# Moving the cluster choice on VectorE to other places in its queue, with its products and the last conversions

## The chip, the cores and the metric

The kernel runs on one core of one Trainium2 chip. The metric is the device time of one execution in microseconds (us), median over runs. Five engines work side by side, each through its own queue in order: PE (TensorE: matmuls and transposes), DVE (VectorE), ACT (ScalarE), POOL (GpSimd), and SP (SyncE), which here only starts DMAs.

## The reference, cut to what matters

Clustered attention over 2 batches, 8 heads, 768 positions of 64, followed by two feed-forward networks (the second one gated). A query only sees the keys of its own cluster:

```python
q_assign = np.argmax(np.einsum('bhsd,hcd->bhsc', q_n, c_n), axis=-1)   # 16 centroids per head
k_assign = np.argmax(np.einsum('bhsd,hcd->bhsc', k_n, c_n), axis=-1)
mask = q_assign[:, :, :, None] == k_assign[:, :, None, :]
scores = np.where(mask, scale * np.matmul(q, k.transpose(0, 1, 3, 2)), -1000000000.0)
attn = np.exp(scores - np.max(scores, axis=-1, keepdims=True))
attn = attn / (np.sum(attn, axis=-1, keepdims=True) + 1e-09)
x = np.matmul(attn, v)
...
h = x @ w_in;  x = (h * (1.0 / (1.0 + np.exp(-h)))) @ w_out
gate = 1.0 / (1.0 + np.exp(-(x @ w_gate)));  out = gate * (x @ w_val) @ w_out
```

## The kernel before

**Pairs and tiles.** Attention runs over 8 pairs (a batch and two heads, p = 0 to 7), a pair over 12 tiles of 128 queries: tiles i = 0 to 5 belong to the first head, named 0_0 to 0_5, tiles 6 to 11 to the second, 1_0 to 1_5. Every product is done from high and low parts. A tile goes through this chain: scores s (PE, L442, four matmuls into one of two PSUM buffers), their negated maximum nm (DVE, L450), the exponential e with the row's sum into tot (ACT, L455), six transposes of e (PE: two into u, L469, and four into t, L478), and copies of u and t into the ring ph (L66, L63; u on DVE, t on DVE or ACT). After three tiles a value group v is done (PE, 12 matmuls, L486); its halves are added by way of other (ACT, L495) and xf (DVE, L498). There are two buffers for s, so the scores of a tile wait for the exponential two tiles back.

**The order on PE** is written by hand (`tc.manual_schedule`): one_tile issues the scores of tile i+2, a due value group at every third tile, pieces of the next pair's preparation, the transposes of tile i, and a step of finishing the previous pair. The table PIECES says how many pieces go ahead of and behind the transposes of each tile. The order on the other engines is decided by the scheduler; `tc.issue_after(x)` keeps an instruction behind x. The list maxima holds all nm, 12 to a pair: index 0 is nm_0_0, index 4 nm_0_4, index 7 nm_1_1, index 11 nm_1_5.

**Preparing the next pair (prep)**, piece by piece: splits of q and k into high and low parts (POOL), products with the centroids pm (PE) and their scaled copy sim (ACT, L271), similarities ps (PE, L162) and a second copy into sim (ACT, L63), and then the *choice* on DVE: mk, the largest similarity of each position (L406); eq, where it is (L409); wq, eq times a rank (L412); the largest of those into mk again (L414), named mk2 below; oh, the one-hot choice (L416). The choice is transposed to pt (PE, L425), copied to rows (ACT, L427) and brought into the mask rows of q and k by four DMAs (L429, L430). The scores of the next pair need these rows.

**Finishing a pair (finish)**: tot + 1e-9 and its reciprocal rs (DVE, L504, L506), a transpose pr (PE, L508), rt (ACT, L510), out to DRAM and back as a broadcast rb (two DMAs, L577, L579), and the product acc (POOL, L516), which is the pair's part of the MLP's input.

**The last pair** has nothing to prepare. There the first MLP weights are converted: converted() takes 64-bit words from DMA tiles (ri, ro) by an ACT operation (L679), a clamp on POOL (L680) and three DVE operations (L685, L687, L689). The first four such tiles are ci_0, ci_1, co_0 and co_1; the list behind ties each of their 12 DVE operations to one maximum of the last pair. From ci_0 and ci_1 come sums si (POOL, L724 to L727) and high and low parts wi0a, wi0b, wi0s, wi0t (high: ACT, L63; low: POOL, L697), from co the parts wo. Behind 255 us only the MLPs run.

Of the kernel before, what the change touches and what calls it, by code (L numbers as in the profile page):

```python
# [15 lines left out]
ALU = mybir.AluOpType  # L16
AX = mybir.AxisListType
# [14 lines left out]
def clustered_attention_then_two_mlps(ctx, tc, qT, kT, v, cen, cenT, w1i, w1o, w2g, w2v, w2o, out):  # L32
    nc = tc.nc
    B, HP, _, S = qT.shape
    D = cen.shape[2]
    H = 2 * HP
    C = cenT.shape[3]
# [70 lines left out]
    with ExitStack() as att:  # L108
# [259 lines left out]
        def prep(p):  # L368
# [34 lines left out]
            yield  # L403
            W = 4 * NT
            sg = sim.rearrange("p t n j c -> p (t n j) c")
            nc.vector.tensor_reduce(mk[:, 0, :], sg, axis=AX.X, op=ALU.max)  # L406
            yield
            eq = wk.tile([P, W, C], BF16, tag="eq", name=f"eq{p}", bufs=1)
            nc.vector.tensor_tensor(eq, sg, mk[:, 0, :].unsqueeze(2).to_broadcast([P, W, C]), op=ALU.is_equal)  # L409
            yield  # L410
            wq = wk.tile([P, W, C], BF16, tag="wq", name=f"wq{p}", bufs=1)
            nc.vector.tensor_tensor(wq, eq, mk[:, 2, 0:C].unsqueeze(1).to_broadcast([P, W, C]), op=ALU.mult)  # L412
            yield
            nc.vector.tensor_reduce(mk[:, 1, :], wq, axis=AX.X, op=ALU.max)  # L414
            o = oh[p % 2]
            nc.vector.tensor_tensor(  # L416
# [83 lines left out]
        def finish(p):  # L500
# [3 lines left out]
            nc.vector.tensor_scalar_add(t, t, 1e-9)  # L504
            rs = fin.tile([P, 2 * NT], F32, tag="rs", name=f"rs{p}")
            nc.vector.reciprocal(rs, t)  # L506
# [87 lines left out]
        def finishing(n):  # L594
            for _ in range(n):
                work[:] = [w for w in work if next(w, work) is not work]

        def pieces(n):
            for _ in range(n):
                next(nxt, None)  # L600

        def gated_start(p, n):
            return tc.issue_after(maxima[1].ins) if p == 0 and n < 6 else nullcontext()

        def due(p, n):
# [7 lines left out]
            ((2, 0), (0, 0), (1, 1), (1, 0), (1, 1), (0, 1), (0, 1), (0, 1), (1, 0), (0, 0), (0, 0), (0, 0)),  # L613
            ((0, 0), (1, 0), (1, 1), (0, 1), (0, 1), (0, 1), (0, 0), (1, 0), (0, 0), (0, 0), (0, 0), (0, 0)),
        )

        def one_tile(p, i, fresh):

            if i == 2 * NT - 2:
                pieces(99)  # L620
                if p + 2 < NPAIR:
                    load(p + 2)
            elif i == 0 and p:
                pieces(1)
            scores(*fresh)
            early, late = PIECES[min(p, 1)][i]
            with gated_start(p, i):
                if i % GT == GT - 1:
                    due(p, i // GT - 1)
                pieces(early)  # L630
                transposes(p, *divmod(i, NT))
                pieces(late)
                finishing(1)
# [34 lines left out]
    behind = maxima[(NPAIR - 1) * 2 * NT :]  # L668
# [475 lines left out]
```

## Time and profile before

| | |
|---|---|
| runs | 789.64, 794.92, 793.48 us; median 793.48 |
| profiled execution | 791.71 us, of which its span 789.9 |
| PE busy | 763.6 us (97% of the span) |
| DVE busy | 636.3 (81%) |
| ACT busy | 395.4 (50%) |
| POOL busy | 397.4 (50%) |
| granted TensorE clock | full speed in all 40 slices |

The attention stage lies between about 10 and 255 us, the period of one of its inner pairs is 29.0 us. Idle time counts where PE has it; the timeline shows in brackets how long an engine stood ahead of an instruction and which instruction released it.

### The profile page before, as it was taken

The page shows a single profiled execution, that of the slowest core. Times are in us where ns is not written, and L with a number is a line of the kernel's source. Part 1 is how long each engine was busy: PE and PEld are TensorE (multiplying, and loading weights), DVE is VectorE, ACT ScalarE, POOL GpSimd, SP SyncE. Part 2 cuts the span into 40 slices and gives each one's busy share as a digit, 9 for nine tenths or more (in the row PEclk, how much of TensorE's full clock was granted, in tenths as well). Part 3 has the DMA queues.
Part 4 walks back from the last instruction along what each step waited for, and adds up shares of the span by engine and source line. Part 5 has one row for each costly group of instructions (what it writes and reads, how often), then busy time and mean ns, then how long its engine had stood idle before and what let it go on. Part 6 is the DMA issues. An engine that isn't in the chain of part 4 may idle for free.

```text
span 789.9 us, 11440 instructions
## 1 busy us (share of the span) xinstructions
PE 763.6 (97%) x4313; PEld 651.5 (82%) x4314; DVE 636.3 (81%) x803; ACT 395.4 (50%) x674; POOL 397.4 (50%) x345
## 2 busy tenths in 40 slices
PE   8899999999979999999999999999999999999998
PEld 4566666766656989989989889998998989999896
DVE  7877787877887899988687778999398796979746
ACT  6657666667666855425236145555532525334120
POOL 5233123457355657656356435446563856839220
PEclk9999999999999999999999999999999999999999
DMA  7575565466421122321121221121221211112004
GB/s 212 134 183 148 133 162 140 122 160 156 120 73 54 54 84 78 133 80 54 59 102 33 74 80 54 55 80 36 72 80 54 80 67 67 54 56 79 1 0 160
DMA packets 25487, 71.60 MB, mean 91 GB/s; under 512 B 4484, under 2 KB 4952, under 8 KB 25432
## 3 DMA queue, kind: packets, MB, share of 16 engines
q1 hardware_dynamic: 24888, 70.84, 30.1%
q8 instruction: 34, 0.56, 0.3%
q14 instruction: 21, 0.17, 0.1%
q10 hardware_dynamic: 544, 0.03, 0.0%
HBM read 48.01 MB, written 3.19 MB: 65 GB/s over the span
## 4 chain that ended last, share of the span: by engine, by line
PE 78%; DVE 12%; ACT 4%; issue 2%; POOL 2%; DMA 1%; SPq 0%; ACTq 0%; POOLq 0%; DVEq 0%
PE z L968 12%; PE v L486 7%; PE s L442 5%; PE h_0x L794 4%; PE h_0w L794 3%; PE y L909 3%; PE g_0w L794 3%; DVE nm L450 3%; PE t L478 3%; PE g_0x L794 2%; PE v_0w L794 2%; PE v_0x L794 2%; PE y_00None L909 2%; PE r L859 2%; PE q L859 2%
## 5 line engine op out<-in xcount | busy, mean ns | idle before, releaser
L455 ACT ACTIVATE e<-s,nm 128x768 f32<-128x768 f32 x96 | 86.4, 900 | 54.1 <-DVE nm L450 53.1
L450 DVE TENSOR_REDUCE nm<-s 128x1 f32<-128x768 f32 x96 | 91.0, 949 | 8.9 <-PE s L442 8.6
L968 PE MATMUL z<-wu,ghb 128*128 128x512 f32 (+1 forms) x292 | 89.5, 388 | 0.5 <-DVE acc L889 0.5
L486 PE MATMUL v<-ph,vv 128*64 128x384 f32 x384 | 69.0, 494 | 0.0
L442 PE MATMUL s<-ka,qa 128*128 128x384 f32 x192 | 57.3, 379 | 10.1 <-ACT e L455 9.8
L968 PEld LDWEIGHTS z<-wu,ghb 128*128 128x128 f32 x292 | 54.1, 188 | 12.4 <-issue 1.3
L478 PE MATMUL t<-ident,e 128*128 128x128 f32 x384 | 58.2, 274 | 3.3 <-DVE ph L66 2.6
L968 PE MATMUL z<-wu,glb 128*128 128x512 f32 (+1 forms) x146 | 56.9, 390 | 0.0
L516 POOL TENSOR_TENSOR acc<-xf,rb 128x768 f32<-128x768 f32 x7 | 12.9, 1836 | 80.5 <-DMA rb<-d_rb 67.2
L442 PE MATMUL s<-k,q 128*128 128x384 f32 x192 | 49.7, 339 | 2.3 <-DMA k<-rows 2.2
L486 PEld LDWEIGHTS v<-ph,vv 128*64 128x64 f32 x384 | 24.7, 136 | 30.7 <-issue 28.8
L478 PEld LDWEIGHTS t<-ident,e 128*128 128x128 f32 x384 | 43.9, 140 | 6.2 <-DVE ph L66 4.4
L889 DVE TENSOR_TENSOR acc<-z,acc 128x1024 f32<-128x1024 f32 (+2 forms) x32 | 36.6, 1153 | 13.5 <-PE z L968 12.9
L469 PEld LDWEIGHTS u<-ident,e 128*128 128x128 f32 x192 | 23.5, 141 | 22.0 <-issue 17.5
L442 PEld LDWEIGHTS s<-ka,qa 128*128 128x128 f32 x192 | 29.0, 190 | 14.4 <-ACT e L455 14.0
L66 DVE COPY ph<-u 128x512 f32<-128x512 f32 x48 | 32.7, 681 | 9.6 <-PE u L469 9.6
L63 ACT ACTIVATE ph<-t 128x512 f32<-128x512 f32 x52 | 30.9, 596 | 18.6 <-PE t L478 17.8
L469 PE MATMUL u<-ident,e 128*128 128x128 f32 x192 | 38.4, 281 | 1.5 <-ACT e L455 1.3
L498 DVE TENSOR_TENSOR xf<-v,other 64x384 f32<-64x384 f32 x32 | 17.7, 553 | 27.5 <-ACT other L495 27.3
L442 PEld LDWEIGHTS s<-k,q 128*128 128x128 f32 x192 | 34.5, 188 | 2.9 <-DMA k<-rows 2.5
L968 PEld LDWEIGHTS z<-wu,glb 128*128 128x128 f32 x146 | 27.4, 188 | 6.9 <-DVE glb L849 1.5
L697 POOL TENSOR_TENSOR wo<-co,wo 128x512 fp32r<-128x512 f32 x16 | 23.2, 1451 | 19.3 <-ACT wo L63 19.2
(626 smaller groups left out, 2161.7 us busy)
## 6 DMA issues: line engine op xcount, KB each, us to landing
ri<-in_w1i SPq DMA_DIRECT2D x16, 512.0 KB, 3.2
ro<-in_w1o SPq DMA_DIRECT2D x16, 512.0 KB, 3.2
ka<-kh SPq DMA_DIRECT2D x32, 192.0 KB, 3.6
rg<-in_w2g SPq DMA_DIRECT2D x12, 512.0 KB, 3.2
rv<-in_w2v SPq DMA_DIRECT2D x12, 512.0 KB, 3.1
ru<-in_w2o SPq DMA_DIRECT2D x12, 512.0 KB, 3.2
qq<-in_qT SPq DMA_DIRECT2D x8, 384.0 KB, 3.3
kk<-in_kT SPq DMA_DIRECT2D x8, 384.0 KB, 4.7
```

The lines of the kernel that those rows point to most:

```text
L66: return nc.vector.tensor_copy(o, i)
L442: nc.tensor.matmul(s[:, g, 0:HS], lhsT=a[:, j, i * P : (i + 1) * P], rhs=c[:, j, g * HS : (g + 1) * HS], start=n == 0, stop=n == 1,)
L450: maxima.append(nc.vector.tensor_reduce(nm, s[:, :, 0:HS], axis=AX.XY, op=ALU.max, negate=True))
L455: x = nc.scalar.activation(e, s[:, :, 0:HS], AF.Exp, bias=nm, scale=1.0, accum_out=tots[p][:, n : n + 1])
L469: nc.tensor.transpose(both[:, kt - 4, i % 2, :], e[:, kt * P : (kt + 1) * P], ident)
L478: nc.tensor.transpose(t[:, kt, :], e[:, kt * P : (kt + 1) * P], ident)
L486: m = nc.tensor.matmul(o[(L, U)[kt % 2]], lhsT=vv[:, j, kt, :], rhs=ring[:, kt, g * G : (g + 1) * G], start=n < 2, stop=n >= NT - 2,)
L794: nc.tensor.matmul(o[:, b, 0:HS], lhsT=w[a][s][:, k, :], rhs=right[b, q][t][:, k, :], start=start and k == 0 and n == 0, stop=k == KQ - 1 ...
L859: nc.tensor.matmul(o[:, h, 0:HS], lhsT=w[f"a{m + 1}{r + 1}"][s][:, k, :], rhs=right[b, f"{r + 1}{h + 1}"][t][:, k, :], start=r == 0 and k ...
L889: nc.vector.tensor_tensor(z, o, z, op=ALU.add)
L909: nc.tensor.matmul(o[:, d, 0:width], lhsT=s[:, d, k, :], rhs=t[:, c], start=k == 0 and m == 0, stop=k == 1 and m == 2,)
L968: nc.tensor.matmul(o[:, a, c], lhsT=s[:, q * P : (q + 1) * P], rhs=r[:, c], start=k == 0 and m == 0, stop=k == 1 and m == 2, skip_group_ch ...
```

## The change

The choice is tied to maxima by queued: mk, eq and wq behind maximum 4 of the pair in progress (7 in pair 0, where p of the prepared pair is 1), mk2 and oh behind maximum 7. The sums tot and rs of a finished pair stand behind maximum 4 of the next one. PIECES has one number for each tile, ahead of the transposes; pm comes at tile 0 and ps at tile 1 (they were at tiles 1 and 2), and the finishing step comes first in a tile's second half. The 12 conversions of the last pair stand three each behind maxima 4, 7, 10 and 11. No instruction is added or taken away.

```diff
             yield
+            def queued(one, *rest, **kw):
+
+                with tc.issue_after(maxima[(p - 1) * 2 * NT + one].ins):
+                    rest[0](*rest[1:], **kw)
+
+            one = 2 * GT + 1 if p == 1 else GT + 1
+            two = 2 * GT + 1
             W = 4 * NT
             sg = sim.rearrange("p t n j c -> p (t n j) c")
-            nc.vector.tensor_reduce(mk[:, 0, :], sg, axis=AX.X, op=ALU.max)
+            queued(one, nc.vector.tensor_reduce, mk[:, 0, :], sg, axis=AX.X, op=ALU.max)
             yield
             eq = wk.tile([P, W, C], BF16, tag="eq", name=f"eq{p}", bufs=1)
-            nc.vector.tensor_tensor(eq, sg, mk[:, 0, :].unsqueeze(2).to_broadcast([P, W, C]), op=ALU.is_equal)
+            most = mk[:, 0, :].unsqueeze(2).to_broadcast([P, W, C])
+            queued(one, nc.vector.tensor_tensor, eq, sg, most, op=ALU.is_equal)
...
-            nc.vector.tensor_tensor(wq, eq, mk[:, 2, 0:C].unsqueeze(1).to_broadcast([P, W, C]), op=ALU.mult)
-            yield
-            nc.vector.tensor_reduce(mk[:, 1, :], wq, axis=AX.X, op=ALU.max)
+            ranks = mk[:, 2, 0:C].unsqueeze(1).to_broadcast([P, W, C])
+            queued(one, nc.vector.tensor_tensor, wq, eq, ranks, op=ALU.mult)
+            yield
+            queued(two, nc.vector.tensor_reduce, mk[:, 1, :], wq, axis=AX.X, op=ALU.max)
             o = oh[p % 2]
-            nc.vector.tensor_tensor(
+            queued(
+                two,
+                nc.vector.tensor_tensor,
...
-            nc.vector.tensor_scalar_add(t, t, 1e-9)
             rs = fin.tile([P, 2 * NT], F32, tag="rs", name=f"rs{p}")
-            nc.vector.reciprocal(rs, t)
+            with tc.issue_after(maxima[(p + 1) * 2 * NT + GT + 1].ins):
+                nc.vector.tensor_scalar_add(t, t, 1e-9)
+                nc.vector.reciprocal(rs, t)
...
         PIECES = (
-            ((2, 0), (0, 0), (1, 1), (1, 0), (1, 1), (0, 1), (0, 1), (0, 1), (1, 0), (0, 0), (0, 0), (0, 0)),
-            ((0, 0), (1, 0), (1, 1), (0, 1), (0, 1), (0, 1), (0, 0), (1, 0), (0, 0), (0, 0), (0, 0), (0, 0)),
+            (2, 0, 2, 1, 1, 4, 0, 1, 0, 0, 0, 0),
+            (1, 1, 3, 0, 0, 1, 0, 1, 0, 0, 0, 0),
         )
...
             scores(*fresh)
-            early, late = PIECES[min(p, 1)][i]
             with gated_start(p, i):
+                finishing(1)
                 if i % GT == GT - 1:
                     due(p, i // GT - 1)
-                pieces(early)
+                pieces(PIECES[min(p, 1)][i])
                 transposes(p, *divmod(i, NT))
-                pieces(late)
-                finishing(1)
...
-    behind = maxima[(NPAIR - 1) * 2 * NT :]
+    behind = [maxima[(NPAIR - 1) * 2 * NT + n] for n in (4, 7, 10, 11) for _ in range(3)]
```

The lines behind L401 move by 10 or 11 in the changed kernel: s is at L453, nm at L461, e at L466, xf at L509, the choice at L407 throughout.

DVE in pair 2, from the maximum of tile 0_4 on, in the kernel before:

```order
L450 TENSOR_REDUCE nm_0_4_1037<-s_0_4_1032 128x1
L498 TENSOR_TENSOR xf_805<-v_1_1_1041,other_1_1_1048 64x384
L406 TENSOR_REDUCE mk<-sim_972 128x24
L66 COPY ph<-t_0_2_1059 128x4x128
L409 TENSOR_TENSOR eq_1091<-sim_972,mk 128x384
L450 TENSOR_REDUCE nm_0_5_1078<-s_0_5_1073 128x1
L66 COPY ph<-u_0_2_1056 128x2x256
L412 TENSOR_TENSOR wq_1116<-eq_1091,mk 128x384
L450 TENSOR_REDUCE nm_1_0_1103<-s_1_0_1098 128x1
```

and the same place in the changed kernel:

```order
L461 TENSOR_REDUCE nm_0_4_1042<-s_0_4_1037 128x1
L407 TENSOR_REDUCE mk<-sim_972 128x24
L517 TENSOR_SCALAR tot_595<-tot_595 128x12
L407 TENSOR_TENSOR eq_1057<-sim_972,mk 128x384
L518 RECIPROCAL rs_1079<-tot_595 128x12
L407 TENSOR_TENSOR wq_1059<-eq_1057,mk 128x384
L509 TENSOR_TENSOR xf_805<-v_1_1_1046,other_1_1_1053 64x384
L66 COPY ph<-t_0_2_1064 128x4x128
L461 TENSOR_REDUCE nm_0_5_1075<-s_0_5_1070 128x1
L66 COPY ph<-u_0_2_1061 128x2x256
```

mk, eq, wq and the two operations of the sums have moved from several places to directly behind nm_0_4; the next maximum has one copy and xf ahead of it.

POOL in the last pair, from the clamp of co_0 on, before (acc is the product of the pair before the last):

```order
L680 TENSOR_SCALAR co_0_3033<-co_0_3033 128x512
L724 TENSOR_TENSOR si_3017<-ci_1_3008 128x256
L726 TENSOR_TENSOR si_3017<-ci_0_3000,ci_1_3008 128x256
L697 TENSOR_TENSOR wi0b<-ci_1_3008,wi0b 128x512
L725 TENSOR_TENSOR si_3017<-si_3017,ci_0_3000 128x256
L516 TENSOR_TENSOR acc<-xf_2486,rb_2738 128x2x384
L727 TENSOR_TENSOR si_3017<-ci_0_3000,si_3017 128x256
```

and changed:

```order
L690 TENSOR_SCALAR co_0_3033<-co_0_3033 128x512
L528 TENSOR_TENSOR acc<-xf_2486,rb_2747 128x2x384
L734 TENSOR_TENSOR si_3017<-ci_1_3008 128x256
L736 TENSOR_TENSOR si_3017<-ci_0_3000,ci_1_3008 128x256
L707 TENSOR_TENSOR wi0b<-ci_1_3008,wi0b 128x512
L735 TENSOR_TENSOR si_3017<-si_3017,ci_0_3000 128x256
L737 TENSOR_TENSOR si_3017<-ci_0_3000,si_3017 128x256
```

acc, which reads the broadcast rb, has moved ahead of all four sums.

ACT in the last pair, before, from the conversion of co_1 on:

```order
L679 ACTIVATE co_1_3044<-ro_1_3042 128x512
L63 ACTIVATE ph<-t_0_5_2785 128x4x128
L63 ACTIVATE wi0s<-si_3017 128x512
L455 ACTIVATE e_1_2_2798,tot_2610<-s_1_2_2791,nm_1_2_2796 128x768
L63 ACTIVATE wo_0_3039<-co_0_3033 128x512
L63 ACTIVATE ph<-t_1_1_2821 128x4x128
L63 ACTIVATE wi0t<-si_3017 128x512
L455 ACTIVATE e_1_3_2816,tot_2610<-s_1_3_2809,nm_1_3_2814 128x768
```

and changed:

```order
L689 ACTIVATE co_1_3044<-ro_1_3042 128x512
L63 ACTIVATE wi0s<-si_3017 128x512
L466 ACTIVATE e_1_4_2834,tot_2610<-s_1_4_2827,nm_1_4_2832 128x768
L63 ACTIVATE wi0t<-si_3017 128x512
L506 ACTIVATE other_0_1_2843<-v_0_1_2836 64x384
L63 ACTIVATE ph<-t_1_2_2849 128x4x128
L63 ACTIVATE wo_0_3039<-co_0_3033 128x512
L63 ACTIVATE ph<-t_1_3_2867 128x4x128
L466 ACTIVATE e_1_5_2862,tot_2610<-s_1_5_2855,nm_1_5_2860 128x768
```

co_1, wi0s and wi0t, which stood ahead of e_1_2 and e_1_3, now stand two tiles later, ahead of e_1_4 and e_1_5.

## Rows read from the trace of the kernel before

**Rows 1.** Busy time by stretches: stretch, its length, busy time and count per engine, clock.

```profile
81.00:110.00 29.00, 27.84 (x188) 19.36 (x187) 23.20 (x36) 19.11 (x39) 7.88 (x6) 1.00 0.57 144
```

**Rows 2.** Timeline of PE in pair 2: start, duration, instruction, idle before and releaser.

```profile
77.10 0.59 PE L442 MATMUL s<-ka,qa 128*128 128x384 f32 x2
...
80.06 0.55 PE L162 MATMUL ps<-ident,sim 128*128 128x128 f32 x3
80.45 0.38 PE L469 MATMUL u<-ident,e 128*128 128x128 f32 x2
...
85.03 0.62 PE L442 MATMUL s<-ka,qa 128*128 128x384 f32 x2 [0.75 <-ACT e L455]
...
88.65 0.59 PE L442 MATMUL s<-ka,qa 128*128 128x384 f32 x2
...
90.00 0.60 PE L442 MATMUL s<-ka,qa 128*128 128x384 f32 x2
...
91.70 0.66 PE L478 MATMUL t<-ident,e 128*128 128x128 f32 x4 [0.17 <-DVE ph L66]
92.11 0.59 PE L442 MATMUL s<-ka,qa 128*128 128x384 f32 x2
```

**Rows 3.** Timeline of DVE, pair 2 (first row: end of the pair before).

```profile
70.74 0.46 DVE L504 TENSOR_SCALAR tot<-tot 128x12 f32<-128x12 f32 x1
...
78.08 0.96 DVE L450 TENSOR_REDUCE nm<-s 128x1 f32<-128x768 f32 x1 [0.44 <-PE s L442]
80.75 0.56 DVE L498 TENSOR_TENSOR xf<-v,other 64x384 f32<-64x384 f32 x1 [1.71 <-ACT other L495]
81.35 0.55 DVE L406 TENSOR_REDUCE mk<-sim 128x24 f32<-128x384 f32 x1
...
82.54 0.55 DVE L409 TENSOR_TENSOR eq<-sim,mk 128x384 bf16<-128x384 f32 x1
83.00 0.95 DVE L450 TENSOR_REDUCE nm<-s 128x1 f32<-128x768 f32 x1
```

**Rows 4.** Timeline of ACT, pair 2.

```profile
80.75 0.49 ACT L63 ACTIVATE sim<-ps 128x384 f32<-128x384 f32 x1
...
83.99 0.90 ACT L455 ACTIVATE e<-s,nm 128x768 f32<-128x768 f32 x1 [0.42 <-DVE nm L450]
```

**Rows 5.** Timelines of PE and of DVE, first pair.

```profile
31.72 0.62 PE L442 MATMUL s<-ka,qa 128*128 128x384 f32 x2 [0.44 <-ACT e L455]
...
39.80 0.63 PE L442 MATMUL s<-k,q 128*128 128x384 f32 x2 [2.21 <-DMA k<-rows]
...
29.70 0.94 DVE L450 TENSOR_REDUCE nm<-s 128x1 f32<-128x768 f32 x1
```

**Rows 6.** Timeline of PE, last pair.

```profile
224.63 0.62 PE L442 MATMUL s<-ka,qa 128*128 128x384 f32 x2 [3.07 <-ACT e L455]
...
232.96 0.66 PE L478 MATMUL t<-ident,e 128*128 128x128 f32 x4 [1.52 <-DVE ph L66]
...
247.85 0.44 PE L469 MATMUL u<-ident,e 128*128 128x128 f32 x2 [1.31 <-ACT e L455]
```

**Rows 7.** Timeline of DVE, last pair.

```profile
221.74 0.82 DVE L685 TENSOR_SCALAR ci<-ci 128x512 int32<-128x512 int32 x1 [2.01 <-POOL ci L680]
...
223.47 0.68 DVE L687 SCALAR_TENSOR_TENSOR ci<-ri,ci 128x512 int32<-128x512 int32 x1
...
227.93 1.80 DVE L687 SCALAR_TENSOR_TENSOR ci<-ri,ci 128x512 int32<-128x512 int32 x1
```

**Rows 8.** Timeline of POOL, last pair.

```profile
227.89 1.29 POOL L697 TENSOR_TENSOR wi0a<-ci,wi0a 128x512 fp32r<-128x512 f32 x1 [5.61 <-ACT wi0a L63]
...
233.76 1.47 POOL L697 TENSOR_TENSOR wi0b<-ci,wi0b 128x512 fp32r<-128x512 f32 x1
...
237.41 1.85 POOL L516 TENSOR_TENSOR acc<-xf,rb 128x768 f32<-128x768 f32 x1 [1.48 <-DMA rb<-d_rb]
```

**Rows 9.** Timeline of ACT, last pair.

```profile
229.71 0.25 ACT L510 ACTIVATE rt<-pr 12x128 f32<-12x128 f32 x1
```

## The prediction

> **What bounds the kernel now.** I read the busy time by stretches first [rows 1]: in one period of a pair of heads, 81 to 110 us, PE is busy 27.84 of 29.00 us, DVE 23.20, ACT 19.11. So PE sets the pace; what the attention stage can give back is the 1.2 us per pair in which PE stands, and whatever stands at its two ends. Then I read where PE stands, in the timeline of PE in one pair [rows 2]: 0.75 us ahead of s at 85.03, released by the exponential on ACT, and 0.17 us ahead of t at 91.70, released by a copy on DVE. Last I followed those waits back on DVE [rows 3]. DVE stands idle 1.71 us ahead of xf at 80.75, while PE does a value group, and directly afterwards it is short of time: mk at 81.35, a copy, eq at 82.54, and only then the maximum nm at 83.00, 5.90 us after s_0_4 started at 77.10. The exponential that needs this nm starts at 83.99 [rows 4], and its s buffer is what PE waits for at 85.03. So work for the *next* pair (mk, eq) delays a maximum that PE needs soon, just behind a gap that would have held it.
>
> The first and the last pair have stalls of their own. First pair [rows 5]: 0.44 us ahead of s at 31.72 and 2.21 us at 39.80, where the next pair's first scores wait for the mask rows, which come out of the cluster choice. Last pair [rows 6]: 3.07 us ahead of s at 224.63, 1.52 at 232.96, 1.31 at 247.85. The cause of the 3.07 is on DVE [rows 7]: the conversion at 221.74 waits 2.01 us for POOL, and the nm behind it, which PE needs, waits too. The MLP stage behind 255 us is the same code before and after; I count it at nothing.
>
> **The change, part by part.** All sums are against the profiled execution: 791.71 us, a span of 789.9 and 1.8 around it. It lies 1.8 below the median of the runs shown, 793.48.
>
> *Pairs 1 to 6, choice on DVE.* No instruction is added; mk, eq, wq and the two small operations of the sums (tot, rs) move ahead of xf, behind the maximum of s_0_4. I call the start of s_0_4 S. The similarities ps, 0.38 us of PE's time (80.06 to 80.45, [rows 2]), now stand ahead of s_0_4, so S comes 0.38 later. On DVE nm starts at S+0.98 as now (77.10 to 78.08), and the next operations take turns after 0.87 (nm), 0.46 (mk), 0.36 (tot), 0.46 (eq), 0.20 (rs, estimated at half of tot) and 0.46 (wq, sized like eq): the durations of [rows 3] less the overlap of 0.09 that eq at 82.54 and nm at 83.00 show. So xf starts at S+3.78; now it is at S+3.65, so the six operations just fit into the idle 1.71 us plus the time that they took later. Then the copy of t_0_2 and at S+4.85 nm_0_5 (now S+5.90); its scores are there at about S+4.55 (2.96 to the end of the value group, 0.6 for the transposes, 0.98 as above), so it is 0.3 late. ACT first copies t_0_3, so the exponential starts at S+6.17, and s_1_1 1.04 later as now (83.99 to 85.03, [rows 2, 4]), at S+7.21, where it now stands at S+7.93. Less the 0.38 of ps: gain 0.34 per pair. Bounds: nothing, if nm_0_5 stays as late as now, and 0.75, the idle in the row.
>
> Further on, mk2 and oh stand behind maximum 7, no longer in the way of the copy that t at 91.70 waits for. From s at 88.65 to s at 92.11 it is 3.46 us now [rows 2]; undisturbed it would be twice a tile of 1.35 (88.65 to 90.00) and pt, taken at ps's 0.38, so 3.08. Of the 0.38 I take 0.33, the end that the free DVE is nearest to; bounds 0 and 0.38. Per pair 0.67, six pairs: **−4.0 us**, bounds 0 and −7.
>
> *First pair.* PE loses 0.68 us at 31.72 (the idle 0.44 and a slower start) and some 2.3 at 39.80 now [rows 5]. Changed, pt stands one tile and a value group earlier, but it has to wait for oh, which for pair 1 stands behind maximum 7: nm at 29.70 becomes 29.85, and 0.87 (nm), 0.60 (a copy) and 0.55 (oh) later it is 31.87. PE, walked through its new order, is there at 30.5, so this costs a new wait of 1.4. In exchange the mask rows land some 1.3 us before they are needed. 0.68 + 2.3 − 1.4: **−1.6 us**, bounds 0 (PE waits as long for pt as it did for rows) and −3.0.
>
> *Last pair.* Conversions came one behind each maximum; now ci_0's three come behind maximum 4, so nothing of POOL's lateness stands ahead of the maxima 0 to 4. The 3.07 becomes the 0.2 that a pair's s always waits there: −2.9. The 1.52 at 232.96 goes with the conversion of 1.80 at 227.93 [rows 7], which now stands behind maximum 7, next to a value group, and with smaller waits on the way I count −4.9 by then (4.4 from these two rows). But the change moves something that it does not name. On POOL the multiplication acc of pair 6 now stands ahead of the four sums si, and of the low half wi0b; before, three of them were ahead of it. acc waits for a broadcast by DMA that starts from rt. acc starts 7.70 us behind rt now (229.71 to 237.41) [rows 8, 9]; rt moves with the pair by 3.1 to 226.6, so acc to 234.3, and it ends 1.8 later, 236.1. Two sums (half as wide as wi0b's 1.47, so 0.7 each) and wi0b bring POOL to 238.95. On ACT the order is now e_1_3, co_1, wi0s, e_1_4, wi0t, other, ph, wo, ph, e_1_5, and co_1 and wi0s wait for POOL here. So e_1_4 and e_1_5, which PE needs, queue behind POOL's wait for a DMA: co_1, wi0s and wi0t 0.65 each (the copy of 384 columns, 0.49 in [rows 4], scaled to 512, an estimate), e twice about 1.0, and four of about 0.5: 5.9 in all, that is 244.8, and PE's transposes of e_1_5 at 244.9 against 247.85 now [rows 6]. Of the 4.9 only **−2.9 us** is left; bounds −0.9 (the broadcast lands 2 us later than that) and −4.9 (nothing held).
>
> Sum: −4.0 − 1.6 − 2.9 = −8.5, so 783.2 for the profiled execution and 793.5 − 8.5 = **785.0** for the median.
>
> One row shows an effect that could touch the conversions and eq and wq alike: the same conversion took 0.68 us at 223.47, and 1.80 at 227.93 [rows 7], while POOL did its two-input subtraction of 1.29 us from 227.89 [rows 8]. The Trainium skill, "SBUF — State Buffer", section "Who interferes with whom", says that a DVE instruction which reads two SBUF inputs and a GpSimd instruction which reads SBUF keep each other out; these two rows agree. By this rule eq and wq would each be up to 1.8 us late wherever POOL does a two-input operation like acc's of 1.85 [rows 8] beside them; in two of six pairs that would take back 2 × 1.8 = 3.6 and give some 788.6, near rival 2 below. The sum above does not contain it, since in the pair of [rows 3] POOL stands idle in that stretch.
>
> **The rivals.** (1) *ACT is not held at the end*: the broadcast lands earlier, or the conversion on ACT is scheduled late without harm. For it: no row tells how much of the 7.70 is the transfer itself. Against: ACT takes its instructions in order, and e_1_4 stands behind wi0s. Then −10.5 in all, 783.0. (2) *The steady pairs gain nothing*: the work in the value stretch makes nm_0_5 as late as before, by 0.67 us more than I walked (a slower operation next to POOL would do). For it: the walk already has nm_0_5 0.28 late. Against: DVE is idle 1.71 us there. Then 1.6 + 2.9 = −4.5, 789.0. (3) *The last pair gains nothing*: POOL's wait for the broadcast grows to eat all 2.9. Then −5.6, 787.9. (4) *Slower*: DVE works in order, so mk right behind nm_0_4 can hold xf, the copy of t_0_2 and nm_0_5 if its input, the second copy of the similarities on ACT, is late. Now ps at 80.06 is followed by its copy at 80.75, 0.49 long [rows 2, 4]; changed, ps starts 1.0 ahead of S, the copy ends near S+0.17, and mk wants it at S+1.85: a margin of 1.7. From 1.4 us beyond that margin in each of six pairs the 8.5 are gone, from 2.7 the kernel is over 1% slower; at 2.8 it would be +8.3, about 802. Against: ACT is busy only 19.11 of 29.00.
>
> **How the numbers follow.** The forecast 785.0, with its own range of 783 to 787, has 0.44; not held 0.17; steady pairs nothing 0.21; last pair nothing 0.11; slower 0.07. From 780.5 (all bounds partly better) to 790.5 (above rivals 2 and 3) this leaves out the slow rival and little else. A measurement of this kernel tells about 1% from no change, as the three runs differ by 0.7%; that is 785.5 and 801.4. The forecast is just beyond it, so of its 0.44 some 0.26 count as faster; of (1) 0.16, of (2) and (3) 0.04. Faster 0.46, slower 0.07, same the rest.
>
> **What would show it.** In a steady pair: idle of PE ahead of s_1_1 down from 0.75 to about 0.4 and none ahead of t behind pt; xf without 1.71 us of idle time; no idle of DVE ahead of mk (rival 4 would show it there). In the first pair: the 2.21 us for rows gone, about 1.4 ahead of pt. In the last: no 3.07 us, but ACT idle behind e_1_3, released by POOL, and POOL idle ahead of acc, released by the DMA. The prediction is wrong if the pair's period does not fall below 29.0 by some 0.6 us, or if the last pair's end moves by less than 1 or more than 4 us, or if the MLP stage, taken as unchanged, changes.

## The result, and the profile after

| | before | changed |
|---|---|---|
| median, us | 792.69 (789.64 to 794.92, 4 runs) | 783.03 (782.44 to 784.39, 4 runs) |
| ratio | | 0.9883, 95% interval 0.9846 to 0.992 |
| profiled execution, us | 791.71, span 789.9 | 784.39, span 782.6 |
| mean granted TensorE clock in it | 1.0 | 0.997 |

The kernel is 9.7 us faster, 1.2%. The prediction was 785.0 with a range of 780.5 to 790.5. The total is near; one term of the sum was mis-sized, as shown below.

First the busy time by stretches over one period of an inner pair, which answers [rows 1] (its length, then busy time and count of PE, PE's weight loads, DVE, ACT, POOL):

```profile
79.50:107.83 28.33, 27.69 (x189) 19.42 (x188) 23.63 (x36) 18.90 (x38) 7.88 (x6) 1.00 0.58 148
```

The period is 28.33 us where it was 29.03 (both from a score to the same score of the next pair), and PE's work is the same but for the edges; 0.64 us of standing are left. PE's timeline in pair 2 of the changed kernel, the place of [rows 2]:

```profile
75.00 0.49 PE L162 MATMUL ps<-ident,sim 128*128 128x128 f32 x3
...
75.90 0.60 PE L453 MATMUL s<-ka,qa 128*128 128x384 f32 x2
...
80.98 0.66 PE L489 MATMUL t<-ident,e 128*128 128x128 f32 x4 [0.22 <-DVE ph L66]
...
83.22 0.61 PE L453 MATMUL s<-ka,qa 128*128 128x384 f32 x2 [0.21 <-ACT e L466]
...
86.82 0.59 PE L453 MATMUL s<-ka,qa 128*128 128x384 f32 x2
...
89.89 0.59 PE L453 MATMUL s<-ka,qa 128*128 128x384 f32 x2
```

s_1_1 now stands 7.32 us behind s_0_4 (75.90 to 83.22), with a wait of 0.21 where it was 0.75; from s_1_2 to s_1_4 it takes 3.07 where it took 3.46, and the wait behind pt is gone. A new small wait of 0.22 stands at 80.98, for DVE's copy of t_0_2. DVE in the same place, which answers [rows 3]:

```profile
76.89 0.96 DVE L461 TENSOR_REDUCE nm<-s 128x1 f32<-128x768 f32 x1
77.88 0.55 DVE L407 TENSOR_REDUCE mk<-sim 128x24 f32<-128x384 f32 x1
78.35 0.16 DVE L517 TENSOR_SCALAR tot<-tot 128x12 f32<-128x12 f32 x1
78.46 0.56 DVE L407 TENSOR_TENSOR eq<-sim,mk 128x384 bf16<-128x384 f32 x1
78.94 0.22 DVE L518 RECIPROCAL rs<-tot 128x12 f32<-128x12 f32 x1
79.08 0.54 DVE L407 TENSOR_TENSOR wq<-eq,mk 128x384 bf16<-128x384 bf16 x1
79.64 0.56 DVE L509 TENSOR_TENSOR xf<-v,other 64x384 f32<-64x384 f32 x1
80.24 0.69 DVE L66 COPY ph<-t 128x512 f32<-128x512 f32 x1
80.84 0.95 DVE L461 TENSOR_REDUCE nm<-s 128x1 f32<-128x768 f32 x1
...
85.20 0.55 DVE L407 TENSOR_REDUCE mk<-wq 128x24 f32<-128x384 bf16 x1
...
87.28 0.54 DVE L509 TENSOR_TENSOR xf<-v,other 64x384 f32<-64x384 f32 x1
```

The 1.71 us ahead of xf are filled without a gap: nm at S+0.99, xf at S+3.74 (walked: 3.78) and nm_0_5 at S+4.94 (walked: 4.85). Nothing waits for the copy of the similarities: mk follows nm at once, so rival 4 did not occur.

The last two rows belong to the second gain, ahead of s_1_4. In the kernel before the same two operations, mk2 and xf, stood later against the maxima:

```profile
86.40 0.54 DVE L414 TENSOR_REDUCE mk<-wq 128x24 f32<-128x384 bf16 x1
86.86 0.94 DVE L450 TENSOR_REDUCE nm<-s 128x1 f32<-128x768 f32 x1
...
90.51 0.54 DVE L498 TENSOR_TENSOR xf<-v,other 64x384 f32<-64x384 f32 x1
```

There mk2 was ahead of nm_1_1 (86.86). The exponential of that tile then started at 87.90 and kept ACT from other until 88.92, xf came behind the next maximum, nm_1_2, and the copy for which PE waited at 91.70 came behind xf. In the changed kernel mk2 is behind nm_1_1, other starts at 86.37, and xf is ahead of nm_1_2 (87.81).

In the first pair, which answers [rows 5], PE waits for oh ahead of pt, and the 2.21 us for the mask rows are gone:

```profile
32.30 0.51 PE L436 MATMUL pt<-identb,oh 128*128 128x128 bf16 x6 [1.19 <-DVE oh L407]
...
39.99 0.62 PE L453 MATMUL s<-ka,qa 128*128 128x384 f32 x2 [0.21 <-ACT e L466]
```

PE at the end of the last pair, which answers [rows 6]:

```profile
217.30 0.62 PE L453 MATMUL s<-ka,qa 128*128 128x384 f32 x2 [0.24 <-ACT e L466]
...
237.21 0.44 PE L480 MATMUL u<-ident,e 128*128 128x128 f32 x2 [0.92 <-ACT ph L63]
238.22 0.66 PE L489 MATMUL t<-ident,e 128*128 128x128 f32 x4 [0.57 <-ACT ph L63]
239.10 0.65 PE L480 MATMUL u<-ident,e 128*128 128x128 f32 x2 [0.23 <-ACT e L466]
239.40 2.27 PE L804 MATMUL h_0x<-x,wi0a 128*128 128x384 f32 x6
```

The 3.07 us have become 0.24. But the six matmuls h_0x took 2.27 us, where the same six took 1.30 before. The busy time by stretches shows why (PE's granted clock is the fraction in front of the last two numbers):

```profile
238.00:239.00 1.00, 0.66 (x4) 0.42 (x4) 1.00 (x3) 1.00 (x4) 0.95 (x1) 1.00 0.90 365
239.00:240.00 1.00, 0.90 (x4) 0.91 (x5) 1.00 (x2) 0.54 (x2) 0.97 (x1) 0.59 0.01 4
240.00:241.00 1.00, 1.00 (x5) 1.00 (x4) 1.00 (x3) 0.00 (x0) 1.00 (x2) 0.50 0.00 0
241.00:242.00 1.00, 1.00 (x6) 0.90 (x5) 1.00 (x2) 0.00 (x0) 1.00 (x2) 0.50 0.00 0
242.00:243.00 1.00, 1.00 (x7) 0.49 (x7) 0.08 (x1) 0.44 (x1) 1.00 (x1) 0.71 0.00 0
```

Right behind the three waits the clock is granted at half, 1.2 GHz, over some 3.4 us, which takes about 1.7 us of PE's clock (0.41, 0.50, 0.50 and 0.29 in the four rows). From the scores s_1_5 to the first of the MLP's products p it took 19.06 us here, and 17.5 to 18.0 in e1, e3, e6, e9 and e10 below, which kept the full clock there: 1.0 to 1.5 us more. This execution lies 1.8 to 2.0 us above the two shortest.

Where the time came from, as the lead of the changed kernel's PE over the kernel before at the same scores, from s_0_1 of the first pair on (the changed profile started 0.48 us later there, ahead of any changed instruction):

| stretch | forecast | measured |
|---|---|---|
| first pair | −1.6 | −1.33 |
| pairs 1 to 4 | −0.67 each | −0.69 each |
| pairs 5 and 6 | −0.67 each | −0.47 and −0.43 |
| last pair, to s_1_1 | −4.9 | −4.68 |
| last pair, given back by the transposes of e_1_5 | 2.0 | 0.43 |
| half clock behind them | none | 1.0 to 1.7 in this execution |

### The profile page after: what moved, and what is told of

Same layout as the page of the kernel before. It is cut to its first block, busy times and chain, and to the rows that moved or that the text cites. A ratio compares the mean times of both kernels' runs of the same rounds, so it can differ in the third digit from the quotient of the medians.

```text
span 782.6 us, 11452 instructions
## 1 busy us (share of the span) xinstructions
PE 764.6 (98%) x4313; PEld 653.6 (84%) x4314; DVE 637.3 (81%) x803; ACT 393.5 (50%) x674; POOL 398.1 (51%) x345
## 4 chain that ended last, share of the span: by engine, by line
PE 83%; DVE 8%; ACT 5%; POOL 1%; issue 1%; DMA 1%; ACTq 0%; DVEq 0%
PE z L978 12%; PE v L497 7%; PE s L453 7%; PE t L489 4%; PE h_0x L804 4%; PE h_0w L804 3%; PE y L919 3%; PE g_0w L804 3%; PE g_0x L804 2%; PE v_0w L804 2%; PE v_0x L804 2%; PE u L480 2%; ACT e L466 2%; PE y_00None L919 2%; PE r L869 2%; PE q L869 2%
## 5 line engine op out<-in xcount | busy, mean ns | idle before, releaser
L466 ACT ACTIVATE e<-s,nm 128x768 f32<-128x768 f32 x96 | 86.3, 901 | 29.7 <-DVE nm L461 29.4
L461 DVE TENSOR_REDUCE nm<-s 128x1 f32<-128x768 f32 x96 | 91.4, 953 | 6.4 <-PE s L453 4.7
L453 PE MATMUL s<-ka,qa 128*128 128x384 f32 x192 | 57.4, 380 | 4.0 <-ACT e L466 4.0
L453 PE MATMUL s<-k,q 128*128 128x384 f32 x192 | 49.6, 338 | 0.1
L453 PEld LDWEIGHTS s<-ka,qa 128*128 128x128 f32 x192 | 29.0, 190 | 8.5 <-ACT e L466 8.4
L453 PEld LDWEIGHTS s<-k,q 128*128 128x128 f32 x192 | 34.6, 188 | 0.6 <-ACT q L322 0.3
L919 PE MATMUL y<-gha,wo 128*128 128x384 f32 x128 | 32.8, 334 | 0.0
L66 DVE COPY ph<-t 128x512 f32<-128x512 f32 x44 | 30.0, 681 | 3.3 <-PE t L489 3.1
```

The costliest lines, as they stand in the source:

```text
L66: return nc.vector.tensor_copy(o, i)
L453: nc.tensor.matmul(s[:, g, 0:HS], lhsT=a[:, j, i * P : (i + 1) * P], rhs=c[:, j, g * HS : (g + 1) * HS], start=n == 0, stop=n == 1,)
L461: maxima.append(nc.vector.tensor_reduce(nm, s[:, :, 0:HS], axis=AX.XY, op=ALU.max, negate=True))
L466: x = nc.scalar.activation(e, s[:, :, 0:HS], AF.Exp, bias=nm, scale=1.0, accum_out=tots[p][:, n : n + 1])
L919: nc.tensor.matmul(o[:, d, 0:width], lhsT=s[:, d, k, :], rhs=t[:, c], start=k == 0 and m == 0, stop=k == 1 and m == 2,)
```

## The experiments

Medians are compared with runs of the kernel before on the same chip: 793.45 for the first four kernels, 793.76 for the next four, 792.80 for the last four.

| kernel | median, us | ratio to before (95%) |
|---|---|---|
| e1_last_only | 789.22 | 0.9949 (0.9932 to 0.9966) |
| e2_choice_only | 787.15 | 0.9927 (0.9912 to 0.9942) |
| e3_xf_late | 779.66 | 0.9829 (0.9814 to 0.9844) |
| e4_casts_late | 782.53 | 0.9877 (0.9852 to 0.9902) |
| e5_no_queue | 788.18 | 0.9929 (0.9908 to 0.9950) |
| e6_sums_free | 783.83 | 0.9880 (0.9860 to 0.9900) |
| e7_split_four | 794.06 | 1.0008 (0.9998 to 1.0019) |
| e8_both | 782.79 | 0.9867 (0.9850 to 0.9885) |
| e9_xf_again | 781.76 | 0.9861 (0.9839 to 0.9884) |
| e10_old_places | 785.25 | 0.9906 (0.9882 to 0.9930) |
| e11_pt_late | 780.95 | 0.9849 (0.9825 to 0.9873) |
| e12_again (the changed kernel) | 784.20 | 0.9888 (0.9866 to 0.9909) |

### Two parts, one at a time

e1_last_only, from the kernel before:

```diff
-    behind = maxima[(NPAIR - 1) * 2 * NT :]
+    behind = [maxima[(NPAIR - 1) * 2 * NT + n] for n in (4, 7, 10, 11) for _ in range(3)]
```

> The kernel before with only the list of maxima for the last pair's 12 conversions changed (three each behind maxima 4, 7, 10 and 11). Theory (the parts add up, and the last pair's part is worth what its stretch shows after the change, -2.85 us): about 789.9 us, and in the trace the wait of 3.07 us ahead of s_0_4 in the last pair falls to about 0.2, with PE 4.7 us ahead by s_1_1 and some 1.8 of it lost again by the last value groups. Rival (the wait of 3.07 comes from POOL being late against PE, which the earlier pairs' change also moves): the wait stays above 1 us and the gain is under 1.5, so above 791.2.

e2_choice_only is the changed kernel with the reverse of these two lines.

> The changed kernel with the old list for the conversions (one behind each maximum of the last pair). Theory (parts add up): -1.3 in the first pair and -3.7 in the pairs 1 to 6, so about 787.7 us, and the wait ahead of s_0_4 of the last pair stays near 3 us. Rival (parts interact): POOL's chain ends at a fixed time or the conversions run into the moved choice, so the wait is over 4 us or under 2 us and the time lies beyond 789 or below 786.

The medians allow that the parts add up: −4.2 and −6.3 make −10.5, the whole −9.7 with an interval of 3 us either way (and −8.6 in e12). PE's timelines say it more sharply: e1 gains 4.54 us in the last pair up to s_1_1 where the changed kernel gains 4.68, and from the first pair to the last e2's lead over the kernel before grows by as much as the changed kernel's, to within 0.03 us. PE's waits ahead of s_0_4 of the last pair, first in e1, then DVE's cause and PE's wait in e2:

```profile
223.76 0.62 PE L442 MATMUL s<-ka,qa 128*128 128x384 f32 x2 [0.37 <-ACT e L455]
```

```profile
216.67 0.82 DVE L695 TENSOR_SCALAR ci<-ci 128x512 int32<-128x512 int32 x1 [1.87 <-POOL ci L690]
```

```profile
219.56 0.62 PE L453 MATMUL s<-ka,qa 128*128 128x384 f32 x2 [2.93 <-ACT e L466]
```

With the new list alone the 3.07 us are gone; with the choice alone they stay, 2.93, and so does the conversion that waits for POOL. e1 gained 4.2, not the expected 2.9: that expectation took the give-back from one profile of the changed kernel, in which most of it was the clock.

### The inner pairs: which move does what

e5_no_queue, from the changed kernel:

```diff
-                with tc.issue_after(maxima[(p - 1) * 2 * NT + one].ins):
-                    rest[0](*rest[1:], **kw)
+                rest[0](*rest[1:], **kw)
```

> The changed kernel in which mk, eq, wq, mk2 and oh are no longer tied to maxima 4 and 7: PE's new order, the sums behind maximum 4 and the last pair's list stay. On DVE mk then stands ahead of nm_0_4, and mk2 and oh ahead of nm_0_5. Theory (where the choice stands against nm_0_4 and nm_0_5 decides the steady pairs' gain): nm_0_5 comes about 1.0 us later than in the changed kernel, and with it s_1_1, in each of six pairs: +6, about 789, and nothing else of the change is lost. Rival (DVE has 0.3 to 1.7 us of idle time around there that takes it, and PE's new order was what mattered): within 1.5 us of 783.

DVE in pair 2 of this kernel, and PE's wait at s_1_1:

```profile
81.23 0.56 DVE L406 TENSOR_TENSOR oh<-wq,mk 128x384 bf16<-128x384 bf16 x1
81.82 0.96 DVE L460 TENSOR_REDUCE nm<-s 128x1 f32<-128x768 f32 x1
```

```profile
83.86 0.61 PE L452 MATMUL s<-ka,qa 128*128 128x384 f32 x2 [1.17 <-ACT e L465]
```

Without the tie the whole choice, mk2 and oh too, stands ahead of nm_0_5 (81.82, S+5.83; in the changed kernel S+4.94), mk even ahead of nm_0_4, and PE waits 1.17 us. By PE's timeline that is 0.55 us in each of four pairs and 0.8 to 1.0 in the last two, 4.1 in all: the theory's mechanism at two thirds of its price, since the copy of t_0_2 comes earlier here and takes 0.4 back. All of it is lost at s_1_1; from s_1_2 to s_1_4 PE is as fast as in the changed kernel.

e10_old_places is the changed kernel with the old places of pm, ps and pr for the pairs 1 to 6:

```diff
-            (1, 1, 3, 0, 0, 1, 0, 1, 0, 0, 0, 0),
+            ((0, 0), (1, 0), (1, 1), (0, 1), (0, 1), (0, 1), (0, 0), (1, 0), (0, 0), (0, 0), (0, 0), (0, 0)),
...
-                finishing(1)
...
+                pieces(late)
+                finishing(1)
```

> The changed kernel with PE's places of pm, ps and pr in the pairs 1 to 6 as before (pm at tile 1, ps at tile 2 behind the value group, the finishing step last in a tile); mk, eq and wq stay tied behind maximum 4, mk2 and oh behind maximum 7. ps then comes too late for mk to stand ahead of xf, and mk, eq and wq fall back to their old places on DVE; mk2 and oh stay behind maximum 7. Theory (two separate gains in a pair: 0.29 us at s_1_1 from the choice's first part in the value stretch, which needs PE's new places, and 0.40 at s_1_4 from mk2 and oh behind maximum 7, which does not): a pair's period rises by 0.3 in each of six pairs, +1.8, about 784.8. Rival (mk waits for the second copy of the similarities with the queue behind it): +1 or more in each pair, over 789.

Its PE row at s_1_1 of pair 2:

```profile
83.35 0.62 PE L453 MATMUL s<-ka,qa 128*128 128x384 f32 x2 [0.76 <-ACT e L466]
```

The wait of 0.75 is back, and only that: 0.30 us in each of the first four pairs, 1.3 in all; the 0.40 behind pt stayed gained, and 785.25 against 784.20 fits. So a pair has two gains of separate origin, as the prediction had them: 0.3 from mk, eq and wq in the value stretch (the time in which PE does a value group), which needs PE's new places, and 0.4 with mk2 and oh behind maximum 7. No run takes the 0.4 away. It is there too in e5, where mk2 stands far ahead of nm_1_1; in all kernels that have it mk2 is not right ahead of nm_1_1 and xf is ahead of nm_1_2, in the kernel before and e1 it is the other way round. So the tie to maximum 7 is one way to get it, and mk2's place as its cause is read from the rows, not tried alone.

e6_sums_free undoes one part, the place of tot and rs:

```diff
-            with tc.issue_after(maxima[(p + 1) * 2 * NT + GT + 1].ins):
+            with nullcontext():
```

> The changed kernel in which tot and rs of a finished pair are no longer tied behind maximum 4 of the next; they then stand at the next pair's start, as before. Theory: tot and rs cost 0.4 us of the value stretch where xf has to wait for ACT's other anyway, so at most -0.15 us for each of the pairs 1 to 4; in the pairs 5 and 6, where tot took 0.44 to 0.47 us beside a subtraction on POOL in place of 0.16, eq with its two inputs in SBUF is held by the same subtraction instead of tot. In all 782 to 783. Rival (only tot, by its form, is held by POOL): the pairs 5 and 6 gain 0.3 each too, and the time is under 782.

PE's timeline differs from the changed kernel's by less than 0.1 us at every score, an offset of 0.42 us at the start taken off. Moving the sums was worth nothing either way. (The median, 783.83, is above the expected 782 to 783; two of its four executions had a mean clock of 0.997.) The theory for the pairs 5 and 6 held: eq, which takes 0.56 in pair 2 of the changed kernel, took 0.84 and 0.69 us beside POOL's subtractions, which ended at 163.50 and 191.97. In pair 6:

```profile
191.69 0.69 DVE L407 TENSOR_TENSOR eq<-sim,mk 128x384 bf16<-128x384 f32 x1
```

### What POOL holds up

In the pairs 5 and 6 the gain was 0.2 to 0.3 smaller. DVE and POOL in pair 6 of the changed kernel:

```profile
191.91 0.47 DVE L517 TENSOR_SCALAR tot<-tot 128x12 f32<-128x12 f32 x1
192.30 0.55 DVE L407 TENSOR_TENSOR eq<-sim,mk 128x384 bf16<-128x384 f32 x1
```

```profile
190.53 1.82 POOL L75 TENSOR_TENSOR xt<-xt,xt 128x768 fp32r<-128x768 f32 x1
```

tot took 0.47 us instead of 0.16, up to the end of POOL's subtraction (190.53 + 1.82 = 192.35). e7_split_four puts such subtractions beside the choice in every inner pair:

```diff
-            on_pool["split", p] = nc.gpsimd.tensor_tensor(kl, kk, kh, op=ALU.subtract)
+            for _ in range(4 if p > 1 else 1):
+                on_pool["split", p] = nc.gpsimd.tensor_tensor(kl, kk, kh, op=ALU.subtract)
```

> The changed kernel in which POOL's subtraction kl of the next pair is done four times in a row (with the same result), so that POOL runs a two-input operation beside mk, tot, eq, rs and wq of each inner pair. Theory (a VectorE operation that needs the port which POOL holds waits for the end of POOL's instruction, and the choice in the value stretch has only 0.1 us to spare): tot lasts until the fourth subtraction ends, 1 to 1.6 us late, and s_1_1 is as much later in four pairs, 1 to 4 us later in the pairs 5 and 6 where POOL has more behind it; +6 to +14, so 789 to 797. Rival (no such holding; 0.44 of tot had another cause): the trace shows tot at 0.2 us and 783 to 784.

DVE and POOL in pair 2 of this kernel:

```profile
80.76 0.55 DVE L408 TENSOR_REDUCE mk<-sim 128x24 f32<-128x384 f32 x1
...
81.35 0.56 DVE L408 TENSOR_TENSOR eq<-sim,mk 128x384 bf16<-128x384 f32 x1
...
81.96 2.05 DVE L408 TENSOR_TENSOR wq<-eq,mk 128x384 bf16<-128x384 bf16 x1
84.04 0.56 DVE L510 TENSOR_TENSOR xf<-v,other 64x384 f32<-64x384 f32 x1
```

```profile
75.75 7.85 POOL L387 TENSOR_TENSOR kl<-kk,kh 128x768 fp32r<-128x768 f32 x4
```

wq took 2.05 us where it takes 0.54, and ended at 84.01, behind the last subtraction (75.75 + 7.85 = 83.60). PE lost 1.5 us in each of four pairs and 1.6 to 1.9 in the pairs 5 and 6, 9.5 in all: the whole gain of the change. The theory's size was right; which operation is hit is set by where the fourth subtraction begins (wq here, not tot). POOL's first three subtractions took 1.82 to 1.84 us, and the fourth, which began at 81.46 while eq ran, 2.13: so DVE seems to hold POOL too, here by 0.3 us (the rest of the 7.85 is gaps of 0.08 between them).

### Further moves

e3_xf_late moves one more operation, from the changed kernel:

```diff
-            nc.vector.tensor_tensor(xf[p][main, g * G : (g + 1) * G], o[main], other[main], op=ALU.add)
+            def added():
+                nc.vector.tensor_tensor(xf[p][main, g * G : (g + 1) * G], o[main], other[main], op=ALU.add)
+
+            if j and g and p < NPAIR - 1:
+                later.append(added)
+            else:
+                added()
...
             scores(*fresh)
+            while later and i == GT:
+                with tc.issue_after(maxima[-1].ins):
+                    later.pop()()
```

> The changed kernel with one more move: in the pairs 1 to 6 the addition xf of the previous pair's last value group stands behind nm_0_5 on DVE, not ahead of the copy of t_0_2. Theory (what is left of the first stall of a pair is DVE reaching the copy of t_0_2 about 0.4 us late, because xf is ahead of it): PE's wait ahead of t_0_3 (0.22 to 0.48 us by the row, about 0.4 with the refill) goes, -0.3 to -0.4 us in each of six pairs, so about 781.0. Rival (the loop of scores, maximum and exponential is the limit there and only its wait grows): the wait of 0.2 ahead of s_1_1 grows by what is saved, and the time stays at 783.

The new wait of 0.22 was real and xf was its cause: every inner pair is 0.43 to 0.45 us shorter (0.3 and 0.7 in the pairs 5 and 6), 2.8 in all. It measured 779.66, and as e9_xf_again, unchanged, 781.76 beside 784.20 for the changed kernel on the same chip: 2.4 less, in executions of which three of five, of either kernel, had a mean clock of 0.997 or 0.998. It beats both kernels. The expectation below was missed on both counts: not 779.7 again but 2.1 more, and 2.4 below the changed kernel, not 2.5 to 3.5. In e9's trace the pairs are worth 2.5 (pair 5 gains 0.1 there), and with full clocks both times it took 780.7 to 781.0 and not 779.6; so the same kernel differed by over 1 us between two chips, for a reason that no run shows.

> The kernel of the run with xf behind nm_0_5, unchanged, once more, beside the changed kernel on the same chip: 779.7 again, and 2.5 to 3.5 us below the changed kernel.

e8_both adds to e3 that nm_1_2 of the first pair stands behind oh.

```diff
-            maxima.append(nc.vector.tensor_reduce(nm, s[:, :, 0:HS], axis=AX.XY, op=ALU.max, negate=True))
+            with tc.issue_after(onehot[1].ins) if (p, j, i) == (0, 1, 2) else nullcontext():
+                maxima.append(nc.vector.tensor_reduce(nm, s[:, :, 0:HS], axis=AX.XY, op=ALU.max, negate=True))
```

> The changed kernel with xf of the last value group behind nm_0_5 (as in the kernel that measured 779.66) and, in the first pair, nm_1_2 behind oh, so that the transposes pt of the choice, for which PE waited 1.19 us, can start earlier. Theory (oh stands behind nm_1_2 and a copy, which is what pt waits for): oh comes about 1.0 us earlier, nm_1_2 0.5 later, the scores s_1_4 behind it gain 0.4 to 0.9, so 778.8 to 779.3. Rival (the maximum nm_1_2 becomes the limit and the tile after it waits for its exponential): no gain, 779.7 or up to 0.5 more.

PE in its first pair:

```profile
31.15 0.51 PE L437 MATMUL pt<-identb,oh 128*128 128x128 bf16 x6 [0.55 <-DVE oh L408]
...
33.62 0.62 PE L454 MATMUL s<-ka,qa 128*128 128x384 f32 x2 [1.30 <-ACT e L468]
```

The rival was right in its mechanism: pt's wait fell from 1.19 to 0.55, and 1.30 us of waiting for an exponential stood in its place; the first pair lost 0.92, where the rival had 0.5 at most. The time, 782.79, cannot be set against e3's 779.66: it is from another chip, and all four executions had a mean clock of 0.997.

e11_pt_late adds to e3 that pt of the first pair comes behind the transposes of tile 1_1.

```diff
-                pieces(PIECES[min(p, 1)][i])
+                at = (p, i) == (0, NT + 1)
+                pieces(0 if at else PIECES[min(p, 1)][i])
                 transposes(p, *divmod(i, NT))
+                pieces(PIECES[0][i] if at else 0)
```

> The kernel with xf behind nm_0_5 and, in the first pair, PE's transposes pt of the choice behind the transposes of tile 1_1 instead of ahead of them. Theory (PE stands 1.19 us ahead of pt for oh, and the transposes of tile 1_1 are ready meanwhile; the mask rows land 1.3 us before they are needed): 0.6 us less, about 779.1, the wait ahead of pt falls to 0.6. Rival (ACT's copy of t_1_1 now stands between and its exponentials come later, or the mask rows come too late): no gain, 779.7 or more.

The wait ahead of pt fell to 0.53, and from s_0_5 to s_1_4 PE gained 0.61 us on the changed kernel, as expected. The median is 780.95, the least on its chip, though 0.8 below e9 is no more than the two kernels' spread.

### The end of the last pair, and the clock

e4_casts_late ties two casts on ACT behind e_1_5:

```diff
-        cast(nc.scalar, hi, src)
+        with tc.issue_after(begin[1].ins) if name in ('i0t', 'o0_0') else nullcontext():
+            cast(nc.scalar, hi, src)
```

(begin[1] is the exponential e_1_5 of the last pair.)

> The changed kernel with the last pair's two casts wi0t and wo_0 on ACT tied behind the exponential e_1_5; nothing else is moved by hand. Theory A (ACT itself is too full there: its casts stand ahead of the copies and of e_1_5 that PE waits for): the waits of 0.92, 0.57 and 0.23 us at the end of the last pair shrink to under 0.8 in sum, TensorE's clock stays granted in full, and the time is 0.5 to 3 us below that of the changed kernel, about 781.8. Theory B (as predicted: POOL's wait for the broadcast holds co_1 and wi0s, and all behind them): e_1_4 starts as late as before, the waits keep more than 1.3 us in sum, and the time is 783.0.

Inconclusive: neither theory's signs all came, and one of the four executions took 786.46. PE's three waits became two, 0.68 and 0.62 us, the clock was granted at 0.999, and the value groups started earlier; but the first product of the MLP that needs wi0s stands 11.66 us behind the scores s_1_5, where it is 11.9 in e1 and e3 with the old casts. 782.53 is what the changed kernel has when its clock is full. The trace does show the hold that theory B speaks of: co_1 and wi0s wait 0.85 and 0.18 us for POOL, and e_1_4 starts at 234.63, where it is 234.53 in the changed kernel.

e12_again is the changed kernel, unchanged, beside these.

> The changed kernel itself once more, on the same chip as the others: 782.5 to 784.5, and of its executions those with TensorE's clock granted in full lie near 782.5 and those with a mean of 0.997 about 1.6 us above (half speed over some 3.3 us behind the waits at the end of the last pair); if the clock has no part in the spread, the two groups do not differ.

Its five executions fall into two groups: 782.53 and 782.60 us with a mean clock of 1.0, and 784.20, 784.27 and 785.06 with 0.997. The kernel before does the same: 790.45 to 791.71 in four executions with 1.0, mostly 792.5 to 794.9 with 0.995 to 0.998. Other kernels do not split so cleanly: e2 took 787.11 us with 0.997 and 787.12 with 1.0, and in the result the changed kernel took 783.44 with 1.0. The profile kept of the kernel before has its full clock throughout, so where it can lose it is seen in e1, which kept the first pair's wait, 2.25 us ahead of 40.04, and in e2, which kept the last pair's, 2.93 ahead of 219.56:

```profile
39.00:40.00 1.00, 0.00 (x0) 0.00 (x0) 0.39 (x2) 0.00 (x0) 0.00 (x0) 1.00 0.47 86
40.00:41.00 1.00, 0.96 (x3) 0.87 (x4) 0.00 (x0) 0.00 (x0) 0.00 (x0) 0.56 0.62 144
```

```profile
219.00:220.00 1.00, 0.44 (x2) 0.44 (x3) 1.00 (x3) 1.00 (x3) 0.00 (x0) 1.00 0.00 0
220.00:221.00 1.00, 1.00 (x6) 0.57 (x6) 1.00 (x2) 0.36 (x1) 0.00 (x0) 0.54 0.00 0
```

In e1 this is clean to read, since up to the last pair its program is the kernel before: PE fell 1.58 us behind the kernel before there. So such a wait costs its own time, and in some executions the half clock behind it as well. The wait alone does not decide it: the kernel before stood 2.21 and 3.07 us with its full clock, and e1 and e3 have the three short waits of the last pair almost as they were (0.93, 0.57, 0.22 and 0.96, 0.57, 0.22) and keep it; what does decide it is open. With full clocks on both sides the change is worth about 8.8 us (791.4 against 782.6, the medians of four executions each with 1.0, over several chips; an estimate). The rest of the 9.7 is probably clock: of the kernel before, 26 of 29 executions beside the experiments had a mean under 0.999, of the changed kernel 4 of 9.

## Why the prediction was right, and where not

**The inner pairs** were right in place and size, 0.69 against 0.67 us in four pairs, and at s_1_1 in mechanism: the walk had xf at S+3.78 and nm_0_5 at S+4.85, and the trace shows 3.74 and 4.94; 0.29 was gained there for 0.34, and e10 takes it away. That the walk came so near is in part luck: from tot to the next operation it took 0.11 us and not 0.36, and the turns of nm and wq were 0.12 and 0.10 longer than counted. The stall did not only shrink, either: of the 0.75, 0.21 are left at s_1_1 and 0.22 stand anew ahead of t_0_3, which the prediction did not name. At s_1_4 0.40 was gained for 0.33, but not because mk2 and oh were in the way of the copy: in the rows of the kernel before they were done by 88.27 and DVE then stood idle twice. The delay went from mk2 over nm_1_1, its exponential, other and xf to the copy.

In the pairs 5 and 6 the sum left POOL out, as the prediction said. It priced what the Trainium skill's rule ("SBUF — State Buffer", "Who interferes with whom") would do at 1.8 us for each such pair. For operations with two inputs in SBUF the traces agree with the rule (eq in e6, wq in e7), and not with that price: the operation is held until POOL's instruction ends, and in the pairs 5 and 6 only 0.3 of it was left. What was held there in the changed kernel is tot, which has one input tensor and of which the prediction did not think. e7 shows nearly the full price, 1.5, where POOL's instruction has only begun.

**The first pair**: the new wait was 1.19 where 1.4 was walked, and the stall of 2.21 went, as forecast. Up to s_1_5 PE lost 0.70 us where 1.4 − 0.68 = 0.72 was walked. The step that was off by 0.3 is the 2.3, of which 2.03 came: once the mask rows are early, the two score buffers make PE wait 0.21 us for an exponential in their place, at 39.99. No run tried this pair's part alone.

**The last pair**, up to s_1_1, was right: 4.68 for 4.9. The step that failed is the size of the hold on ACT, by the 7.70 us at its head. The prediction let acc follow rt by the 7.70 us of [rows 8, 9] and put nine ACT operations behind POOL, which left 2.9 of the 4.9. The rows after (first POOL, then ACT):

```profile
228.58 1.83 POOL L528 TENSOR_TENSOR acc<-xf,rb 128x768 f32<-128x768 f32 x1 [2.63 <-DMA rb<-d_rb]
```

```profile
222.21 0.25 ACT L522 ACTIVATE rt<-pr 12x128 f32<-12x128 f32 x1
...
233.07 0.69 ACT L689 ACTIVATE co<-ro 128x512 f32<-128x512 f32 x1 [0.53 <-POOL wi0b L707]
233.99 0.63 ACT L63 ACTIVATE wi0s<-si 128x512 fp32r<-128x512 f32 x1 [0.23 <-POOL si L735]
...
238.05 0.90 ACT L466 ACTIVATE e<-s,nm 128x768 f32<-128x768 f32 x1
```

acc starts 6.37 us behind rt, not 7.70. The rest of the chain was as forecast: ACT waited for POOL, 0.76 us in all, and from co_1 to the transposes of e_1_5 it is 6.03 us (233.07 to 239.10) where 5.9 were walked. With the 4.50 us of the earlier pairs added back, acc is at 233.1 and not at 234.3, co_1 at 237.6 and not at 238.95, the transposes at 243.6 and not at 244.9: the 1.3 us are there from the first of them on. The transposes stand at 239.10 where they stood at 247.85 [rows 6], 8.75 earlier, 4.25 without the earlier pairs. So 4.25 of the 4.68 were kept, not 2.9, and by the prediction's own sign (the end moves by more than 4 us) the last pair is a miss. What happened lies near rival 1, whose condition, a broadcast that lands earlier, was met, and which had 0.17; but ACT was held. That rival 1's total, 783.0, is the measured one is luck: it had 10.5 us of gain, and the rows of the table give 9.2 ahead of the clock.

Why the broadcast is faster was not tried. By SP's rows its second part (rb) was issued 3.07 us behind rt before, right behind a weight load of 512 KB, and 2.31 after, with the load 3.6 us behind it (at 228.09); that is 0.76 of the 1.33. In the other runs acc starts 6.4 to 7.4 us behind rt, 6.37 and 6.68 in two profiles of the changed kernel, so 7.70 was the longest of all.

**What nobody priced** is the clock. The prediction carried the 1.8 us between the profiled execution and the median along as a constant. By the executions beside the experiments it is about the difference between one of the kernel before with its full clock and one without.

**The total** came out 2.0 us below the forecast. 0.8 of it is the median of the kernel before, which one more run put at 792.69. Of the other 1.2 the hold gives 1.35 and the pairs 1 to 4 give 0.1, less 0.3 in the first pair and 0.4 in the pairs 5 and 6; the 0.5 that is left is put down to the clock, without a run that shows it. So the near total owes something to terms that cancel. Rivals 2 and 3 did not occur, and rival 4 neither: mk follows nm_0_4 at once. The MLP is unchanged: from the first of its products p to the end it takes 528.7 us before and 528.9 after.

## What to carry to other kernels

Find the stretch in which the engine with the late result stands idle, and put the work of the next stage there by hand: behind the result that the critical engine needs now, ahead of the one that it needs next. Then read the queue once more; what had been last in it (here xf) is often the next thing to move, here worth another 2.4 to 2.8 us. And when an order shifts a transfer or another engine's work, look at what it will queue behind, and do not carry its delay along as a constant.

## What the runs showed of the hardware

A wait of PE can cost more than its length: behind waits of 2.25 us (e1) and 2.93 (e2), and behind three short ones of 0.92, 0.57 and 0.23 (the changed kernel), the granted clock was 1.2 GHz for about 3.4 us, and PE came out 1.0 to 1.6 us later. It does not happen behind every such wait: waits as long kept the full clock in the kernel before (2.21, 3.07), in e1 and in e3, and of five executions of the changed kernel in e12 three lost it by their mean. A 128x12 operation of 0.16 us on VectorE and 128x384 ones of 0.54 to 0.56 with two inputs waited for the end of a GpSimd subtraction of 1.82 us (tot 0.44 and 0.47, eq 0.69 and 0.84, wq 2.05); a TENSOR_REDUCE beside the same subtractions kept its 0.55.
